# Moving start-up work of a convolution and feed-forward kernel between VectorE, GpSimd, TensorE and the load queue

## Chip, cores, metric

One Trainium2 chip (trn2), one of its cores. The metric is the device time of one execution in microseconds; the median of several runs is quoted. The kernel before took 696.43 us (696.14 to 696.79, 4 runs).

## The reference

`x` is 8 x 4096 x 192. Each channel is convolved causally along the sequence with 7 taps, the softmax of its head's 7 weights (8 heads of 24 channels). The result passes, as 32768 tokens of 192, through two matrix products with a swish between them.

```python
w = softmax(weight)                                 # 8 heads x 7 taps
x_unf = x_pad[:, arange(S)[:, None] + arange(7)]    # 7 causal positions
conv = einsum('hk,bskhg->bshg', w, x_unf)           # 32768 x 192
h = conv @ w_in                                     # 192 -> 2048
g = h * (1 / (1 + exp(-beta * h)))
out = g @ w_out                                     # 2048 -> 192
```

## The kernel before

The kernel works in stages. A stage handles one chunk of 512 tokens from each of two halves of the batch; the first chunk is cut into two stages of 256 tokens, so that work can begin early. In each stage TensorE runs 16 units: the first-layer products of stage `s` (`hidden`) and the second-layer products of stage `s-1` (`output`). ScalarE applies the swish to each unit. VectorE convolves for the stage after the next, 21 instructions per chunk (7 taps, 3 channel groups of 64), which are queued and popped between units. As g = silu(beta h) / beta, the division is folded into w_out, once, at the start.

The first two stages cannot wait for VectorE's convolution. Theirs is done on TensorE as seven matmuls per channel group, each with a diagonal matrix of one tap's weight (`diag`). The parts that matter (cuts marked):

```python
    steps = [(0, 0, TOK // 2), (0, TOK // 2, TOK // 2)]      # two half chunks
    steps += [(ch, 0, TOK) for ch in range(1, N_CH)]
    psum_h = ctx.enter_context(tc.tile_pool(name="psum_h", bufs=2, space=PSUM))
    psum_o = ctx.enter_context(tc.tile_pool(name="psum_o", bufs=2, space=PSUM))
    # ... cut
    def load_w_in(i):                          # GpSimd queue, cast to bf16
        cols = slice(i * FW, (i + 1) * FW)
        nc.gpsimd.dma_start(out=w_in_s[0:DG, :, cols],
            in_=moe_w_in[:, cols].rearrange("(c d) f -> d c f", c=NG))

    def copy_w_in(i):                          # second half of the partitions
        cols = slice(i * FW, (i + 1) * FW)
        nc.vector.tensor_copy(w_in_s[DG : 2 * DG, :, cols], w_in_s[0:DG, :, cols])
    # ... cut: prologue: fillers, head weights spread to channels, transposes,
    #          diag, the first half chunk's convolution
    def taps():                                # exact taps for VectorE's convolution
        pq = psum_o.tile([128, 2, TOK], FP32, name="po")[:, 0, 0 : NG * (K + 1)]
        spread(pq, sel, e8)                    # fp32: 6 records for 3 matmuls, 0.83 us
    # ... cut
    cast(2)
    for c in range(0, NF, 4):
        prep_w_out(c, 4)                       # nc.gpsimd.tensor_tensor: w_out / beta
    cast(3)
    # ... cut
    first_work = {                             # inserted after unit u of the first stage
        0: lambda: (first_xt(), taps()),
        2: lambda: (more(xt1_work)(), copy_w_in(1)),
        4: lambda: (more(xt1_work)(), copy_w_in(2)),
        6: lambda: (more(conv1_work)(), copy_w_in(3)),
        8: more(conv1_work),
        11: more(conv1_work),
    }
    pops = {1: 12, 2: 26}                      # VectorE taps issued per stage
```

## Time and profile before

| what | before |
|---|---|
| median time | 696.43 us |
| TensorE busy | 687.6 of 695.1 us |
| a unit in the steady stages (16 first-layer units and 16 second-layer blocks a stage) | 0.65 + 0.66 us |
| first activation of the first stage | 11.84 us |
| start of ScalarE's unbroken run (13th unit of the first stage) | 23.05 us |
| first activation of the third stage | 37.18 us |
| TensorE's end | 690.99 us |

The profile's first part gives busy time by engine. Of the kernel before:

```profile
PE 687.6 (99%) x11467; PEld 526.6 (76%) x11467; DVE 551.4 (79%) x938; ACT 580.0 (83%) x546; POOL 70.0 (10%) x83
```

TensorE is full. From the third stage on only its matmuls matter, and the change touches none of them. What can move is the start. The next view is ScalarE's timeline: start, length, engine, line, operation, shape, count, and in brackets how long the engine stood idle before the group and for whom.

```profile
11.84 0.69 ACT L402 ACTIVATE g<-ph,beta 128x512 bf16<-128x512 f32 x1 [0.37 <-PE ph L395]
13.49 2.55 ACT L402 ACTIVATE g<-ph,beta 128x512 bf16<-128x512 f32 x4 [0.97 <-PE ph L395]
16.25 1.27 ACT L402 ACTIVATE g<-ph,beta 128x512 bf16<-128x512 f32 x2 [0.21 <-PE ph L395]
18.09 1.43 ACT L402 ACTIVATE g<-ph,beta 128x512 bf16<-128x512 f32 x2 [0.57 <-PE ph L395]
20.30 1.97 ACT L402 ACTIVATE g<-ph,beta 128x512 bf16<-128x512 f32 x3 [0.78 <-PE ph L395]
23.05 13.11 ACT L402 ACTIVATE g<-ph,beta 128x512 bf16<-128x512 f32 x20 [0.78 <-PE ph L395]
37.18 1.11 ACT L402 ACTIVATE g<-ph,beta 128x1024 bf16<-128x1024 f32 x1 [1.02 <-PE ph L395]
```

Sixteen activations of 0.655 us make up the first stage. The five gaps between them sum to 3.31 us (0.97 + 0.21 + 0.57 + 0.78 + 0.78). Each follows work that `first_work` inserts on TensorE; with two PSUM buffers, `hidden` is never more than about one unit ahead. From 23.05 us on ScalarE runs without a gap through the whole second stage, and so does TensorE. Before 37.18 us it waits 1.02 us for the third stage. The chain of waits (start, length, engine, tile, line) shows what was late there:

```profile
15.81 0.96 DVE xt L346
...
16.80 3.05 DVE w_in_s L172 x2
...
19.88 2.92 DVE ct L376 x3
22.79 1.32 DVE ct L378 x2
...
32.66 3.98 DVE ct L378 x6
...
36.69 0.39 PE ph L395 x2
```

The chain runs on VectorE for 21 us: two copies of w_in, first taps, other taps. TensorE's last two matmuls of the third stage's first unit start at 36.69 us, when VectorE's last tap is ready. The two copies take 3.05 us, while one alone takes 0.69 us at 8.77 us: at 16.2 to 22.4 us GpSimd runs its four products for w_out:

```profile
16.22 6.16 POOL L352 TENSOR_TENSOR w_out_s<-w_out_raw,beta_r 128x768 bf16<-128x768 f32 x4 [2.48 <-DMA w_out_raw<-in_moe_w_out_dram]
```

### The profile page before, as it was taken

How to read it: one execution, taken by the hardware profiler on the slowest of the kernel's cores; microseconds unless marked ns; L12 is line 12 of the kernel's file. 1: busy time of each engine (PE TensorE's matmuls, PEld its weight loads, DVE VectorE, ACT ScalarE, POOL GpSimd, SP SyncE). 2: the span in 40 equal slices, each digit the busy share in tenths (PEclk: the TensorE clock that was granted, in tenths of full speed). 3: DMA queues.
4: the chain of work that ended last, by engine and by line, in shares of the span. 5: the costliest groups of instructions: out<-in, count | busy, mean ns of one | idle time of the engine just before them, and what ended most of it. 6: DMA issues, size and time to landing. Idle time of an engine off the chain costs nothing.

```text
span 695.1 us, 24865 instructions
## 1 busy us (share of the span) xinstructions
PE 687.6 (99%) x11467; PEld 526.6 (76%) x11467; DVE 551.4 (79%) x938; ACT 580.0 (83%) x546; POOL 70.0 (10%) x83
## 2 busy tenths in 40 slices
PE   9999999999999999999999999999999999999997
PEld 6867777777777777777777777777777777777777
DVE  5999998998777987777987777987778987777222
ACT  6898888888888888888888888888888888888881
POOL 7934455000000000000000000000000000000000
PEclk9999999999999999999999999999999999999999
DMA  9999999922232022222023222032222122211012
GB/s 193 144 159 159 168 177 171 123 63 70 54 65 71 27 68 72 47 70 70 26 71 70 49 70 70 25 71 70 48 71 55 40 70 71 48 48 48 25 48 70
DMA packets 181497, 54.57 MB, mean 79 GB/s; under 512 B 146432, under 2 KB 181072, under 8 KB 181392
## 3 DMA queue, kind: packets, MB, share of 16 engines
q0 software_dynamic: 98048, 14.89, 29.8%
q1 hardware_dynamic: 83296, 38.09, 23.9%
q8 instruction: 89, 1.46, 0.9%
q14 instruction: 16, 0.13, 0.1%
q10 hardware_dynamic: 48, 0.01, 0.0%
HBM read 28.98 MB, written 37.29 MB: 95 GB/s over the span
## 4 chain that ended last, share of the span: by engine, by line
PE 96%; DVE 3%; ACT 0%; issue 0%
PE po L442 48%; PE ph L395 46%; DVE ct L378 2%; PE ph L256 0%; DVE w_in_s L172 0%; DVE ct L376 0%; PE ph L205 0%; PE po L209 0%; PE po L243 0%; ACT g L402 0%; PE po L256 0%; DVE xt L346 0%; DVE osb L457 0%; DVE ct L327 0%; ACT xt_145 L269 0%
## 5 line engine op out<-in xcount | busy, mean ns | idle before, releaser
L402 ACT ACTIVATE g<-ph,beta 128x1024 bf16<-128x1024 f32 (+1 forms) x528 | 572.7, 1090 | 96.7 <-PE ph L395 92.6
L442 PEld LDWEIGHTS <-g 64*128 64x128 bf16 x8192 | 369.2, 94 | 101.9
L442 PE MATMUL po<-w_out_s,g 64*128 64x192 bf16 x8192 | 429.8, 243 | 0.0
L395 PE MATMUL ph<-ct,w_in_s 64*128 64x512 bf16 (+1 forms) x3168 | 426.2, 370 | 2.0 <-ACT g L402 1.1
L378 DVE SCALAR_TENSOR_TENSOR ct<-xt,cw,ct 128x512 bf16<-128x512 bf16 x558 | 379.4, 745 | 0.0
L395 PEld LDWEIGHTS <-w_in_s 64*128 64x128 bf16 x3168 | 162.5, 94 | 56.4 <-issue 2.9
L456 DVE COPY osb<-po 128x384 f32<-128x384 f32 x127 | 70.8, 558 | 126.9 <-PE po L442 120.7
L457 DVE TENSOR_TENSOR osb<-po,osb 128x384 f32<-128x384 f32 x129 | 71.5, 555 | 6.0 <-ACT osb L454 1.6
L95 POOL DMA_DIRECT2D xd<-in_x_dram x60 | 54.4, 909 | 46.1 <-DMA xd<-in_x_dram 42.3
L376 DVE TENSOR_SCALAR ct<-xt,cw 128x512 bf16<-128x512 bf16 x93 | 29.5, 372 | 0.0
L454 ACT COPY osb<-po 128x192 f32<-128x192 f32 x2 | 0.6, 320 | 9.9 <-PE po L442 9.9
L352 POOL TENSOR_TENSOR w_out_s<-w_out_raw,beta_r 128x768 bf16<-128x768 f32 x4 | 6.2, 1568 | 2.5 <-DMA w_out_raw<-in_moe_w_out_dram 2.5
L205 PE MATMUL ph<-zeros 128*128 128x512 bf16 x7 | 3.5, 623 | 1.3 <-DVE warm L129 1.3
L172 DVE COPY w_in_s<-w_in_s 64x1536 bf16<-64x1536 bf16 x4 | 4.4, 1121 | 0.1
L256 PE MATMUL po<-xt_145,diag 128*128 128x256 f32 x28 | 4.4, 296 | 0.0
L256 PEld LDWEIGHTS po<-xt_145,diag 128*128 128x128 f32 x28 | 3.6, 189 | 0.7 <-issue 0.6
L256 PEld LDWEIGHTS ph<-xt_145,diag 128*128 128x128 f32 x14 | 3.1, 327 | 0.6 <-ACT xt_145 L269 0.6
L256 PE MATMUL ph<-xt_145,diag 128*128 128x256 f32 x14 | 3.4, 427 | 0.1
L185 POOL DMA_DIRECT2D w_out_raw<-in_moe_w_out_dram x4 | 3.1, 771 | 0.3 <-DMA x1b<-in_x_dram 0.3
L295 ACT ACTIVATE ct<-po,rn 128x256 bf16<-128x256 f32 x1 | 0.5, 475 | 2.6 <-PE po L256 2.6
L165 POOL DMA_DIRECT2D w_in_s<-in_moe_w_in_dram x4 | 2.7, 669 | 0.0
L205 PEld LDWEIGHTS <-zeros 128*128 128x128 bf16 x7 | 0.8, 126 | 2.3 <-DVE warm L129 1.3
(51 smaller groups left out, 28.1 us busy)
## 6 DMA issues: line engine op xcount, KB each, us to landing
out_dram<-osb SPq DMA_DIRECT2D x60, 384.0 KB, 3.1
xd<-in_x_dram POOLq DMA_DIRECT2D x54, 198.0 KB, 14.5
w_out_raw<-in_moe_w_out_dram POOLq DMA_DIRECT2D x4, 384.0 KB, 9.4
out_dram<-osb SPq DMA_DIRECT2D x7, 192.0 KB, 3.7
xd<-in_x_dram POOLq DMA_DIRECT2D x6, 192.0 KB, 13.7
x_83<-in_x_dram SPq DMA_DIRECT2D x4, 192.0 KB, 2.9
w_in_s<-in_moe_w_in_dram POOLq DMA_DIRECT2D x4, 192.0 KB, 7.7
xt<-xd SPq DMA_TRANSPOSE x30, 5.1
```

The lines of the kernel that those rows point to most:

```text
L95: nc.gpsimd.dma_start(out=xd[r0:, :, h, :], in_=x_v[p, t0:t1, h, :].rearrange("t (c d) -> t c d", c=NG),)
L172: nc.vector.tensor_copy(w_in_s[DG : 2 * DG, :, cols], w_in_s[0:DG, :, cols])
L205: nc.tensor.matmul(pf[:, 0, :], zeros[:, 0:128], zeros, start=True, stop=True)
L256: nc.tensor.matmul(pv, diag[:, c, k, :], xt0[:, c, o : o + n], start=(k == 0), stop=(k == K - 1),)
L352: nc.gpsimd.tensor_tensor(w_out_s[:, c0 : c0 + n, :], w_out_raw[:, c0 : c0 + n, :], beta_r[:, c0 : c0 + n].unsqueeze(2).to_broadcast((128, ...
L376: nc.vector.tensor_scalar_mul(dst, src, scalar)
L378: nc.vector.scalar_tensor_tensor(out=dst, in0=src, scalar=scalar, in1=dst, op0=ALU.mult, op1=ALU.add)
L395: nc.tensor.matmul(ph[:, h, 0:n], w_in_s[rows, j, cols], cts[s][rows, j, 0:n], start=(j == 0), stop=(j == NG - 1),)
L402: nc.scalar.activation(gs[s][:, fc, :, 0:n], ph[:, :, 0:n], AF.Silu, scale=beta[:, fc : fc + 1])
L442: nc.tensor.matmul(po[:, r, b * D : (b + 1) * D], g[rows, fc, h, q * BLK : (q + 1) * BLK], w_out_s[rows, fc, :], start=(fc == 0), stop=(fc ...
L456: nc.vector.tensor_copy(dst, po[:, 0, cols])
L457: nc.vector.tensor_tensor(dst, po[:, 1, cols], dst, ALU.add)
```

## The change

Its stated parts are: w_out scaled on VectorE instead of GpSimd; the last two of four w_in pieces loaded for both halves of the partitions, so VectorE copies two pieces less; and one channel group of the second chunk convolved by diagonals on TensorE, so VectorE has 14 taps instead of 21 there. The diff also moves the insertions of the first stage (after units 1, 2, 5, 8, 11 instead of 2, 4, 6, 8, 11), makes the exact taps from one-pass fp32r matmuls of the residual, puts three small filler matmuls between the first spread matmuls, issues the casts of later chunks at other places, and pops VectorE's first taps after units 3 to 9 of the first stage (before: 6 to 15). The intent is to relieve VectorE, on which the chain runs until 36.7 us. Its core (cut):

```diff
-    for i in range(1, NW):
-        load_w_in(i)
+    load_w_in(1)
+    for i in range(2, NW):
+        for h in range(2):
+            load_w_in(i, h)
@@ prologue
-    spread(pc[:, 0, :], sel_r, e8r)
+    e8l = setup.tile([H, K + 1], FP32R)
+    nc.vector.tensor_tensor(e8l, e8, e8r.bitcast(FP32), ALU.subtract)
+    spread(pc[:, 0, :], sel_r, e8r, between=1)     # a 128-column filler before each
@@ exact taps
-        spread(pq, sel, e8)
+        spread(pq, sel_r, e8l)
+        nc.vector.tensor_tensor(ef, pq.rearrange("p (c k) -> p c k", c=NG), eu, ALU.add)
@@ second chunk, third channel group
+    def second_conv():
+        pv = psum_o.tile([128, 2, TOK], FP32, name="po")[:, 0, :]
+        for k in range(K):
+            o = HALO - PAD + k
+            nc.tensor.matmul(pv, diag[:, 2, k, :], xt1[:, o : o + TOK],
+                             start=(k == 0), stop=(k == K - 1))
+        nc.scalar.mul(cts[2][:, 2, :], pv, rn[:, 2:3])
@@ w_out
-        nc.gpsimd.tensor_tensor(
+        nc.vector.tensor_tensor(
@@ where it is inserted: (stage, unit)
-        2: lambda: (more(xt1_work)(), copy_w_in(1)),
-        4: lambda: (more(xt1_work)(), copy_w_in(2)),
-        6: lambda: (more(conv1_work)(), copy_w_in(3)),
-        8: more(conv1_work),
-        11: more(conv1_work),
+        (0, 1): lambda: (more(xt1_work)(), copy_w_in(1)),
+        (0, 2): more(xt1_work),
+        (0, 5): more(conv1_work),
+        (0, 6): lambda: cast(3),
+        (0, 8): more(conv1_work),
+        (0, 11): lambda: (prep_w_out(0), prep_w_out(4), more(conv1_work)()),
+        (0, 13): lambda: prep_w_out(8),
+        (0, 14): lambda: prep_w_out(12),
+        (0, 15): lambda: cast(4),
+        (1, 7): second_conv,
-    pops = {1: 12, 2: 26}
+    pops = {1: 10, 2: 24}
```

More of the change, by code (lines that the diff above doesn't have):

```diff
@@ L161, with load_w_in @@
     w_in_s = consts.tile([128, NG, F], BF16)
-    def load_w_in(i):
+    def load_w_in(i, h=0):
         cols = slice(i * FW, (i + 1) * FW)
         nc.gpsimd.dma_start(
-            out=w_in_s[0:DG, :, cols],
+            out=w_in_s[h * DG : (h + 1) * DG, :, cols],
             in_=moe_w_in[:, cols].rearrange("(c d) f -> d c f", c=NG),
@@ L201, with fill, spread @@
     pf = psum_h.tile([128, 2, TOK], FP32, name="ph")
-    def fill(n):
+    def fill(n, cols=TOK):
         for _ in range(n):
-            nc.tensor.matmul(pf[:, 0, :], zeros[:, 0:128], zeros, start=True, stop=True)
-    def spread(dst, sel, e8):
+            nc.tensor.matmul(
+                pf[:, 0, 0:cols], zeros[:, 0:128], zeros[:, 0:cols], start=True, stop=True
+            )
+    def spread(dst, sel, e8, between=0):
         for c in range(NG):
+            fill(between, 128)
             nc.tensor.matmul(
@@ L274 @@
     diag_v(1)
+    nc.vector.tensor_copy(x0b[:, HB:NB], x0[:, HB:NB])
     for k in range(K):
@@ L295 @@
             nc.scalar.mul(ct[:, c, 0:n0], pv, rn[:, c : c + 1])
-    beta_r = setup.tile([128, NF], FP32)
-    nc.vector.reciprocal(beta_r, beta)
-    nc.vector.tensor_copy(x0b[:, HB:NB], x0[:, HB:NB])
     cw = consts.tile([128, NG, K], FP32)
@@ L304, in taps @@
         pq = psum_o.tile([128, 2, TOK], FP32, name="po")[:, 0, 0 : NG * (K + 1)]
-        spread(pq, sel, e8)
-        pq = pq.rearrange("p (c k) -> p c k", c=NG)
+        spread(pq, sel_r, e8l)
+        ef = setup.tile([128, NG, K + 1], FP32)
+        nc.vector.tensor_tensor(ef, pq.rearrange("p (c k) -> p c k", c=NG), eu, ALU.add)
         rq = setup.tile([128, NG], FP32)
-        nc.vector.reciprocal(rq, pq[:, :, K])
+        nc.vector.reciprocal(rq, ef[:, :, K])
         nc.vector.tensor_tensor(
-            cw, pq[:, :, 0:K], rq.unsqueeze(2).to_broadcast((128, NG, K)), ALU.mult
+            cw, ef[:, :, 0:K], rq.unsqueeze(2).to_broadcast((128, NG, K)), ALU.mult
         )
@@ L333, in first_conv @@
             yield
+    xt1 = setup.tile([128, HALO + TOK], FP32R)
+    def second_conv():
+        pv = psum_o.tile([128, 2, TOK], FP32, name="po")[:, 0, :]
+        for k in range(K):
+            o = HALO - PAD + k
+            nc.tensor.matmul(
+                pv, diag[:, 2, k, :], xt1[:, o : o + TOK], start=(k == 0), stop=(k == K - 1)
+            )
+        nc.scalar.mul(cts[2][:, 2, :], pv, rn[:, 2:3])
     def second_xt():
@@ L343, in second_xt, with prep_w_out @@
                 nc.vector.tensor_copy(
-                    xt[:, :, HALO - PAD : HALO], xt0[:, :, HALO + TOK - PAD :]
+                    xt[:, 0:2, HALO - PAD : HALO], xt0[:, 0:2, HALO + TOK - PAD :]
                 )
-                nc.vector.tensor_copy(xt[:, :, HALO:], pt)
+                nc.vector.tensor_copy(xt[:, 0:2, HALO:], pt[:, 0:2, :])
+                nc.vector.tensor_copy(
+                    xt1[:, HALO - PAD : HALO], xt0[:, 2, HALO + TOK - PAD :]
+                )
+                nc.vector.tensor_copy(xt1[:, HALO:], pt[:, 2, :])
             yield
     w_out_s = consts.tile([128, NF, D], BF16)
-    def prep_w_out(c0, n):
-        nc.gpsimd.tensor_tensor(
-            w_out_s[:, c0 : c0 + n, :],
-            w_out_raw[:, c0 : c0 + n, :],
-            beta_r[:, c0 : c0 + n].unsqueeze(2).to_broadcast((128, n, D)),
+    beta_r = setup.tile([128, NF], FP32)
+    def prep_w_out(c):
+        if c == 0:
+            nc.vector.reciprocal(beta_r, beta)
+        nc.vector.tensor_tensor(
+            w_out_s[:, c : c + 4, :],
+            w_out_raw[:, c : c + 4, :],
+            beta_r[:, c : c + 4].unsqueeze(2).to_broadcast((128, 4, D)),
             ALU.mult,
@@ L359 @@
     cast(2)
-    for c in range(0, NF, 4):
-        prep_w_out(c, 4)
-    cast(3)
     def conv_ops(s):
@@ L380, in tap @@
                 )
-        return [lambda j=j, k=k: tap(j, k) for k in range(K) for j in range(NG)]
+        return [lambda j=j, k=k: tap(j, k) for k in range(K) for j in range(NG - (s == 2))]
     gs = {}
@@ L468 @@
     first_work = {
-        0: lambda: (first_xt(), taps()),
-        2: lambda: (more(xt1_work)(), copy_w_in(1)),
-        4: lambda: (more(xt1_work)(), copy_w_in(2)),
-        6: lambda: (more(conv1_work)(), copy_w_in(3)),
-        8: more(conv1_work),
-        11: more(conv1_work),
+        (0, 0): lambda: (first_xt(), taps()),
+        (0, 1): lambda: (more(xt1_work)(), copy_w_in(1)),
[8 more added lines that the diff above has]
+        (1, 7): second_conv,
     }
-    pops = {1: 12, 2: 26}
+    pops = {1: 10, 2: 24}
     queue = deque()
@@ L486 @@
                 output(s - 1, u)
-            if s == 0 and u in first_work:
-                first_work[u]()
+            if (s, u) in first_work:
+                first_work[s, u]()
             n = pops.get(s, 24)
-            pops_u = (u + 1) * n // NF - u * n // NF if s else u > 5
+            pops_u = (u + 1) * n // NF - u * n // NF if s else 2 < u < 10
             for _ in range(pops_u):
@@ L493 @@
                     queue.popleft()()
-            if u == 0 and s + 4 < N_CH:
+            if u == 0 and 0 < s < N_CH - 4:
                 cast(s + 4)
```

## The prediction

> **What bounds the kernel now.** TensorE: 687.6 of 695.1 us busy at granted clock 1.00 (busy table). In the steady stages a unit costs 0.65 us of first-layer and 0.66 us of second-layer matmuls without a wait (chain in order of time, from 53 us on). The change touches none of these; only the first 53 us can move. The timeline shows there:
> - 0 to 11.5 us, prologue. 14 conv taps by diagonals from 6.35 take 3.36 us, 7 later ones (16.5) 1.09; their weight loads fall from about 235 to 120 ns at about 10.2 us[...].
> - 11.5 to 25.1, first half chunk: 16 units of 0.655 us on ScalarE, idle 3.3 us in five gaps, each behind TensorE work (transposes, tap matmuls, conv) that two PSUM buffers cannot hide. VectorE delays TensorE little (0.42, 0.27, 0.45 us).
> - 25.1 to 35.6, second half: TensorE and ScalarE both full, 0.655 us a unit.
> - At 35.6 the third stage waits for VectorE's convolution: its first unit is done at 37.08 instead of about 36.23, costing 0.85 us. The chain runs on VectorE from 15.8 to 36.7.
>
> **The change.** VectorE, 15.8 to 36.7: two copies of w_in go (3.04 us, slowed by GpSimd; 0.69 alone), seven taps go (0.35 + 6 x 0.745 = 4.8 us), three first taps fall from 2.92 to about 1 us; four products of 128x768 come (estimate 0.9 each, from the 0.94 us product of that shape). Net about 6 us less: the wait at 35.6 vanishes, 0.85 us gained.
>
> TensorE: seven 512-column fp32r taps in the second half. A 256-column group inserts 1.18 us (16.36 to 17.54); 7 x 0.107 us more make 1.9 us, with ScalarE's scaling of about 0.67 us (from 0.475 us for half) about 2.05 us, all on the chain, as that stage has no slack. Kernel-tap matmuls in one pass instead of two: 0.4 us off. Transposes after units 1 and 2 instead of 2 and 4, waiting for a buffer: by my hand schedule ScalarE's gaps become 3.9 instead of 3.3 us. The three fillers cost up to 0.3 us[...]. The two added loads land near 15 to 17 us, before units 8 and 12; w_out lands 2.3 us later, still before its use.
>
> **Sum.** -0.85 + 2.05 + 0.6 + 0.3 = +2.1 if the clock rises as before[...]. As unseen scheduling gains are likely in a change placed this finely, I lean lower: predicted 697.4 us, 8 in 10 between 695.2 and 699.2. Faster by over 2%: 0.01; within 2%: 0.985; slower: 0.005.
>
> **What would show it.** No convolution wait at the start of the third stage; a hole of about 2 us in ScalarE's run near unit 7 of the second stage, with seven 512-column matmuls in about 1.8 us; w_out products near 0.9 us, first taps near 0.35; ScalarE's gaps in the first stage about 3.9 us; the 1.31 us steady unit unchanged; the first 14 conv taps 3.3 us (cold) or about 2 (warm).
>
> **What would make it wrong.** The clock rising earlier with DMA keeping up; w_out or w_in landing late on the longer GpSimd queue and stalling VectorE; ScalarE's gaps in the first stage shrinking; a wait for a PSUM buffer at unit 8 of the second stage, whose output tile reuses the one being emptied.

Three passages are cut, because they rest on what no trace or run here shows: why the weight loads get shorter, and, in the change and in the sum, that the fillers bring this forward. The sum came to +2.1 us, or to +0.9 with the terms that are cut (the first stage 0.9 us sooner instead of the fillers' 0.3 us); the four terms that stand give +2.1.

Measured numbers beside the rest: in the trace of before the first 14 taps start 213 ns apart and the next seven 120 ns, with weight loads of 330 and 190 ns. "Cold" and "warm" stand for taps before and after that fall, and the clock's rise for the moment at which a trace's clock record begins (9.90 us before); the 2 us for 14 warm taps is about twice the 1.09 us of seven. The 0.107 us for 256 more columns in a matmul became 0.103 us, (1.81 - 1.09) / 7 between the two traces; the one-pass matmuls saved 0.34 us of the 0.4 us said. The 0.3 us for the fillers is the estimate; what they cost is under after_again.

## The result

The changed kernel took 698.75 us (698.47 to 699.11, 4 runs) against 696.43 us: ratio 1.0033, 95% interval 1.0016 to 1.0051. It is slower, by about 2.3 us, though within 2%. A ratio here is the mean time of one kernel's fast runs over that of the other's of the same rounds, so it is not quite the ratio of the medians. Run once more beside others, the changed kernel gave 699.12 us and 1.0038 (1.0026 to 1.0051). Its output was correct, as was that of every kernel below.

Busy times of the changed kernel:

```profile
PE 689.0 (99%) x11474; PEld 528.8 (76%) x11474; DVE 547.1 (78%) x937; ACT 580.0 (83%) x547; POOL 65.1 (9%) x81
```

TensorE is busy 1.4 us longer, VectorE 4.3 us and GpSimd 4.9 us less: the work did leave them. ScalarE's timeline in the changed kernel:

```profile
11.98 0.69 ACT L424 ACTIVATE g<-ph,beta 128x512 bf16<-128x512 f32 x1 [0.37 <-PE ph L417]
13.30 0.69 ACT L424 ACTIVATE g<-ph,beta 128x512 bf16<-128x512 f32 x1 [0.63 <-PE ph L417]
14.46 0.69 ACT L424 ACTIVATE g<-ph,beta 128x512 bf16<-128x512 f32 x1 [0.47 <-PE ph L417]
15.35 1.97 ACT L424 ACTIVATE g<-ph,beta 128x512 bf16<-128x512 f32 x3 [0.20 <-PE ph L417]
18.08 1.97 ACT L424 ACTIVATE g<-ph,beta 128x512 bf16<-128x512 f32 x3 [0.77 <-PE ph L417]
20.83 1.97 ACT L424 ACTIVATE g<-ph,beta 128x512 bf16<-128x512 f32 x3 [0.79 <-PE ph L417]
23.59 7.85 ACT L424 ACTIVATE g<-ph,beta 128x512 bf16<-128x512 f32 x12 [0.79 <-PE ph L417]
32.89 0.69 ACT L351 ACTIVATE ct<-po,rn 128x512 bf16<-128x512 f32 x1 [1.45 <-PE po L348]
33.48 5.25 ACT L424 ACTIVATE g<-ph,beta 128x512 bf16<-128x512 f32 x8
39.08 1.11 ACT L424 ACTIVATE g<-ph,beta 128x1024 bf16<-128x1024 f32 x1 [0.35 <-PE ph L417]
```

The gaps of the first stage now sum to 3.65 us (0.63 + 0.47 + 0.20 + 0.77 + 0.79 + 0.79). The run that was unbroken is broken at 31.44 us: ScalarE waits 1.45 us for seven matmuls and then scales their result (0.69 us). The gap before the third stage is down from 1.02 to 0.35 us, the bare hand-over: only_second_conv and relief_split have 0.35 us there too. The chain of the changed kernel:

```profile
31.04 1.81 PE po L348 x7
...
38.33 0.65 PE ph L417 x6
```

It has left VectorE and runs on TensorE alone: the seven matmuls of the second convolution stand in it with 1.81 us, and the third stage starts with six matmuls in 0.65 us and no wait.

The loss can be split at events that both traces have. "First stage" is from the first activation to the start of the 13th, "second stage" from there to the third stage's first activation, "rest" from there to TensorE's end:

| us | first activation | first stage | second stage | rest | TensorE's end |
|---|---|---|---|---|---|
| before | 11.84 | 11.21 | 14.13 | 653.81 | 690.99 |
| changed | 11.98 | 11.61 | 15.49 | 653.80 | 692.88 |
| difference | +0.14 | +0.40 | +1.36 | -0.01 | +1.89 |

The trace of before is of a run of 696.80 us, that of the changed kernel of one of 698.71 us: their difference of 1.91 us is the traced one. The larger gap of 2.3 us between the medians comes from where other runs of each kernel fell. What their starts scatter with is seen under after_again. The rest of the kernel takes the same time to 0.01 us in both, and to 0.02 us in all but one of the kernels below, so only the first three columns need attention.

### The profile page after: what moved, and what is told of

Read it like the earlier page. It is cut to its first block, busy times and chain, and to the rows that moved or that the text cites. A ratio compares the mean times of both kernels' runs of the same rounds, so it can differ in the third digit from the quotient of the medians.

```text
span 697.0 us, 24878 instructions
## 1 busy us (share of the span) xinstructions
PE 689.0 (99%) x11474; PEld 528.8 (76%) x11474; DVE 547.1 (78%) x937; ACT 580.0 (83%) x547; POOL 65.1 (9%) x81
## 4 chain that ended last, share of the span: by engine, by line
PE 98%; ACT 1%; DVE 0%; issue 0%
PE po L464 48%; PE ph L417 48%; PE po L263 1%; ACT g L424 1%; PE ph L207 0%; PE ph L263 0%; PE po L250 0%; PE po L348 0%; DVE xt L323 0%; PE po L214 0%; ACT xt L276 0%; ACT ct L303 0%; DVE osb L479 0%; ACT osb L476 0%; DVE zeros L127 0%
## 5 line engine op out<-in xcount | busy, mean ns | idle before, releaser
L400 DVE SCALAR_TENSOR_TENSOR ct<-xt,cw,ct 128x512 bf16<-128x512 bf16 x552 | 375.4, 744 | 0.0
L398 DVE TENSOR_SCALAR ct<-xt,cw 128x512 bf16<-128x512 bf16 x92 | 27.4, 351 | 0.2 <-DMA xt<-xd 0.2
L207 PE MATMUL ph<-zeros 128*128 128x512 bf16 (+1 forms) x10 | 4.2, 524 | 1.3 <-DVE warm L129 1.3
L263 PE MATMUL po<-xt,diag 128*128 128x256 f32 x28 | 4.4, 296 | 0.0
L263 PEld LDWEIGHTS po<-xt,diag 128*128 128x128 f32 x28 | 3.6, 189 | 0.7 <-issue 0.6
L377 DVE TENSOR_TENSOR w_out_s<-w_out_raw,beta_r 128x768 bf16<-128x768 f32 x4 | 3.6, 952 | 0.0
L263 PEld LDWEIGHTS ph<-xt,diag 128*128 128x128 f32 x14 | 2.6, 285 | 0.6 <-ACT xt L276 0.6
L263 PE MATMUL ph<-xt,diag 128*128 128x256 f32 x14 | 2.8, 377 | 0.1
```

The source lines that it names most:

```text
L207: nc.tensor.matmul(pf[:, 0, 0:cols], zeros[:, 0:128], zeros[:, 0:cols], start=True, stop=True)
L263: nc.tensor.matmul(pv, diag[:, c, k, :], xt0[:, c, o : o + n], start=(k == 0), stop=(k == K - 1),)
L377: nc.vector.tensor_tensor(w_out_s[:, c : c + 4, :], w_out_raw[:, c : c + 4, :], beta_r[:, c : c + 4].unsqueeze(2).to_broadcast((128, 4, D) ...
L398: nc.vector.tensor_scalar_mul(dst, src, scalar)
L400: nc.vector.scalar_tensor_tensor(out=dst, in0=src, scalar=scalar, in1=dst, op0=ALU.mult, op1=ALU.add)
```

## Experiments

Twelve kernels ran, in three groups, each group on one chip with the kernel before in the same rounds, five rounds each. The two theories at the start: (A) the second convolution costs TensorE and ScalarE about 2 us in a stage where both are full and buys back under 1 us, and the places of the insertions cost a little more; (B) the loss is elsewhere, in the longer load queue, in VectorE's new work, or in the fillers.

| kernel | median us | ratio to before (95%) | first act. | first stage | second stage |
|---|---|---|---|---|---|
| no_second_conv | 698.31 | 1.0028 (1.0014 to 1.0041) | 11.72 | 11.60 | 14.48 |
| no_fill | 697.95 | 1.0026 (1.0013 to 1.0038) | 11.82 | 11.59 | 15.49 |
| old_places | 698.55 | 1.0028 (1.0015 to 1.0040) | 12.09 | 10.52 | 15.49 |
| only_second_conv | 699.32 | 1.0042 (1.0029 to 1.0054) | 12.28 | 12.47 | 15.51 |
| pool_w_out | 699.42 | 1.0042 (1.0029 to 1.0054) | 12.23 | 11.61 | 15.97 |
| old_places_no_conv | 696.52 | 0.9999 (0.9986 to 1.0013) | 12.55 | 10.55 | 13.79 |
| relief_only | 695.29 | 0.9988 (0.9975 to 1.0000) | 11.96 | 10.52 | 14.50 |
| relief_split | 699.60 | 1.0040 (1.0027 to 1.0053) | 12.04 | 10.43 | 17.53 |
| best | 695.54 | 0.9987 (0.9973 to 1.0001) | 11.20 | 10.86 | 13.78 |
| best_fill2 | 695.84 | 0.9986 (0.9973 to 0.9998) | 10.74 | 10.53 | 13.79 |
| only_fill | 696.28 | 1.0002 (0.9990 to 1.0015) | 11.80 | 10.79 | 14.03 |
| after_again | 699.12 | 1.0038 (1.0026 to 1.0051) | 12.44 | 11.60 | 15.49 |

The medians of before were 696.10, 696.46 and 696.57 us in the three groups. The three columns of stages come from one trace of each kernel, and that run need not be a typical one: it was the slowest of the five for no_fill, only_second_conv and relief_only, and the fastest for no_second_conv, old_places, best_fill2 and only_fill.

### no_second_conv

```diff
-        (1, 7): second_conv,
-        return [... for j in range(NG - (s == 2))]
+        return [... for j in range(NG)]          # VectorE has all 21 taps again
-    pops = {1: 10, 2: 24}
+    pops = {1: 15, 2: 26}
```

> The changed kernel with the third channel group of the second chunk given back to VectorE, all else kept. Theory A (the TensorE insertion of 1.94 us in the full second stage is the loss, and it buys back less than 0.9 us): the second stage shrinks to 10.5 us; VectorE ends its 21 taps near 36.9 us, so the third stage waits about 0.8 us and its first unit ends near 37.4 us (38.98 in the changed kernel, 37.08 before). Time about 1.6 us below the changed kernel, 0.2 to 0.4 above the kernel before. Rival B (without the seven taps moved, VectorE is several us late): first unit later than 38.5 us, time as the changed kernel or worse.

ScalarE and VectorE of this kernel around the third stage's start:

```profile
23.32 13.11 ACT L409 ACTIVATE g<-ph,beta 128x512 bf16<-128x512 f32 x20 [0.78 <-PE ph L402]
37.80 9.22 ACT L409 ACTIVATE g<-ph,beta 128x1024 bf16<-128x1024 f32 x9 [1.37 <-PE ph L402]
```

```profile
22.88 0.96 DVE L333 TENSOR_TENSOR ct<-po,rn 128x768 bf16<-128x768 f32 x1 [1.42 <-PE po L263]
...
25.48 4.06 DVE L385 SCALAR_TENSOR_TENSOR ct<-xt,cw,ct 128x512 bf16<-128x512 bf16 x6
30.81 0.56 DVE L463 COPY osb<-po 128x384 f32<-128x384 f32 x1 [1.26 <-PE po L449]
...
31.87 5.38 DVE L385 SCALAR_TENSOR_TENSOR ct<-xt,cw,ct 128x512 bf16<-128x512 bf16 x8
```

The second stage's run is unbroken again, 20 activations in 13.11 us. But VectorE's last tap ends at 37.25 us, and the gap is 1.37 us, that is 1.02 us more than the hand-over of 0.35 us; 0.8 us had been expected. The second stage is 1.01 us shorter than in the changed kernel (15.49 to 14.48), not the 1.6 us that theory A expected of the time. The ratio moved less still (1.0033 and 1.0038 to 1.0028): the intervals overlap, so only the trace tells the two kernels apart. Theory A has the right sign and too large a size: with the insertions and pops at these places VectorE needs much of what TensorE was given. It idles 1.42 us for the last first-stage convolution and 1.26 us for an output block, both in program order ahead of taps that were ready.

### no_fill

```diff
-    spread(pc[:, 0, :], sel_r, e8r, between=1)
+    spread(pc[:, 0, :], sel_r, e8r)              # residual of the taps computed later
```

> The changed kernel without the three small fillers between the spread matmuls, and with the residual of the taps computed later on VectorE. Theory A (fillers delay the first taps by 0.7 us but make the array clock rise about 0.9 us earlier, so they nearly cancel): taps start at 6.4 us instead of 7.06, the clock rises near 10 us again, the first activation near 11.85 instead of 11.98; time 0.1 to 0.2 us lower. Rival B (the clock's rise does not depend on the fillers): rise stays near 9.2 us, first activation near 11.3, time 0.7 us lower.

The stages are those of the changed kernel to 0.02 us. The first taps start at 6.35 us instead of 7.06, take 3.36 us instead of 2.85, and the first activation is at 11.82 instead of 11.98 us, the numbers of theory A. But after_again, the changed kernel itself, had its first activation at 12.44 us, so one pair of traces does not decide this; see there. (By the clock records, which begin at 9.90 us before and at 9.14 us in the changed kernel, the rise is 0.76 us earlier in that pair, not 0.9.) The ratio is not told apart from that of the changed kernel.

### old_places

```diff
-        (0, 1): lambda: (more(xt1_work)(), copy_w_in(1)),
-        (0, 2): more(xt1_work),
-        (0, 5): more(conv1_work),
-        (0, 6): lambda: cast(3),
+        (0, 2): lambda: (more(xt1_work)(), copy_w_in(1)),
+        (0, 4): more(xt1_work),
+        (0, 6): lambda: (more(conv1_work)(), cast(3)),
 # and VectorE's taps popped after units 5 to 11 instead of 3 to 9
```

> The changed kernel with the insertions of the first stage back after units 2, 4 and 6 (instead of 1, 2 and 5). Theory A (these places cost ScalarE about 0.4 us of idle time): the second stage starts near 25.25 us instead of 25.61, its gaps on ScalarE sum to about 3.3 instead of 3.65 us; time 0.3 to 0.4 us lower than the changed kernel. Rival B (the 0.4 us came from VectorE or the longer load queue): start stays near 25.6 us, time the same.

The first stage falls to 10.52 us, 1.08 us less than in the changed kernel where 0.4 had been expected, and its gaps to 2.73 us (0.63 + 0.21 + 0.58 + 0.53 + 0.78). Theory A's sign holds, its size does not, because two gains of the change were hidden under the new places: against the kernel before, the gap behind the exact taps fell from 0.97 to 0.63 us (one pass instead of two, 0.49 us of TensorE instead of 0.83), and one of the gaps of 0.78 us to 0.53, as unit 8 no longer waits for VectorE's copy of w_in (0.42 us in the traced run of the kernel before; only_fill, with the same copies, shows no such wait, so the second gain is not one of every run). The times moved less than the trace, as this kernel's runs fell in two groups, 697.70 and 697.73 us (the profiled one among them), and 698.55 to 698.59 us.

### only_second_conv

```diff
+            if (s, u) == (1, 7):
+                second_conv()                    # the kernel before, plus this alone
-    pops = {1: 12, 2: 26}
+    pops = {1: 10, 2: 24}
```

> The kernel before with only the second convolution by diagonals added, nothing else of the change. Theory A: insertion of 1.95 us in the second stage, the wait of 0.67 to 0.85 us at the third gone: time 1.1 to 1.4 us above the kernel before, that is more than half of the change's whole loss. Rival B (VectorE's relief there pays for the insertion): time equal to the kernel before within 0.3 us.

It is slower by 2.9 us. The second stage is 15.51 us, 1.38 us over the kernel before, which is what theory A expected. The other 1.26 us come in the first stage:

```profile
20.53 0.69 ACT L417 ACTIVATE g<-ph,beta 128x512 bf16<-128x512 f32 x1 [1.32 <-PE ph L410]
```

```profile
PE ph L410 <- DVE w_in_s L172: 1.4, 1, 1.4
```

TensorE waits 1.4 us for VectorE's copy of w_in. Laying out the third channel group in fp32r takes VectorE longer (four copies with 1.94 us in the changed kernel's trace, two with 1.13 us in that of before), and here the copy comes behind that and beside GpSimd's products. The trace is of the slowest of five runs (698.64 to 699.85 us), so this wait may be shorter in others. In the trace, then, the second convolution needs the loads for both halves, and the changed kernel shows that even with them it is a loss.

### pool_w_out

```diff
-        nc.vector.tensor_tensor(                 # the changed kernel, w_out / beta
+        nc.gpsimd.tensor_tensor(                 # on GpSimd again, after the casts
```

> The changed kernel with w_out scaled on GpSimd again, as before the change. Theory A (VectorE idles about 6 us in the changed second stage, so its 3.65 us of products are free there and their move to VectorE neither costs nor gains): time within 0.3 us of the changed kernel, 2.2 to 2.6 us above the kernel before; VectorE's first taps longer than the 0.35 us they take alone. Rival B (GpSimd's products hold VectorE up): first stage 0.5 us or more longer, time as much higher.

Theory A's number falls, by the trace: the second stage is 0.48 us longer than in the changed kernel. The times alone cannot say so, as the intervals overlap (1.0042 against 1.0033 and 1.0038). The rival has the cause right and the place wrong: the first stage, which it expected to be 0.5 us longer, is unchanged (11.61 us). In the groups by shape between 15 and 27 us, the columns after the bar are busy us and mean ns of one. First the changed kernel, then pool_w_out:

```profile
L400 DVE SCALAR_TENSOR_TENSOR ct<-xt,cw,ct 128x512 bf16<-128x512 bf16 x7 | 4.8, 742 | 0.0
L377 DVE TENSOR_TENSOR w_out_s<-w_out_raw,beta_r 128x768 bf16<-128x768 f32 x4 | 3.6, 952 | 0.0
L398 DVE TENSOR_SCALAR ct<-xt,cw 128x512 bf16<-128x512 bf16 x2 | 1.0, 545 | 0.0
```

```profile
L402 DVE SCALAR_TENSOR_TENSOR ct<-xt,cw,ct 128x512 bf16<-128x512 bf16 x7 | 8.4, 1256 | 0.0
L400 DVE TENSOR_SCALAR ct<-xt,cw 128x512 bf16<-128x512 bf16 x2 | 1.9, 973 | 0.0
```

The same seven taps take 1256 ns each instead of 742, the two first taps 973 instead of 545. Seven times 514 ns is 3.6 us, as much as VectorE's own four products cost (3.6 us). VectorE then delivers the second stage's input late, TensorE waits 0.7 us for it, and that is the longer second stage. GpSimd's products run here from 16.83 to 24.19 us, with a break of 0.8 us; the five taps beside and just after them take 7.03 us together, the next four 2.72 us. By what mechanism they slow VectorE no run shows. So scaling w_out on VectorE was a sound part of the change: about 3.6 us are paid on VectorE either way, and there they can be placed.

### old_places_no_conv

This kernel takes the edits of no_second_conv and old_places together, with `pops = {1: 12, 2: 26}` and VectorE's taps popped after units 5 to 15 of the first stage.

> The changed kernel with two parts undone: insertions after units 2, 4 and 6, and no second convolution on TensorE. Theory A (the two losses add, and VectorE with w_out's products ends its taps near 36.0 us): first stage from first activation to ScalarE's unbroken run 10.5 us as in old_places; the third stage still waits for VectorE about 1 us; from the first activation to TensorE's end about 678.6 us (679.15 before, 680.92 in the changed kernel); time 0.2 to 0.6 us below the kernel before. Rival B (VectorE is later than that): at or above the kernel before.

The first stage is 10.55 us and the second 13.79 us, 0.34 us shorter than before; from the first activation to TensorE's end it took 678.15 us, as expected within 0.5 us. Removing these two parts took 1.06 and 1.70 us off the changed kernel's stages, more together than the 1.01 us of no_second_conv might suggest: with these places and pops VectorE idles 0.19 us for the convolution instead of 1.42, and the gap before the third stage is 0.68 us. So these two parts are what makes the changed kernel lose: without them the stretch from the first activation to TensorE's end falls from 680.90 to 678.15 us, 1.00 us under the kernel before (679.15). The traced run is the median one, and in it the first activation came at 12.55 us, the latest of all, which takes back 0.71 us; the other runs were not traced.

### relief_only

```diff
 # on the kernel before
-    for i in range(1, NW):
-        load_w_in(i)                             # and copies 2 and 3 gone
+    load_w_in(1)
+    for i in range(2, NW):
+        for h in range(2):
+            load_w_in(i, h)
-        spread(pq, sel, e8)                      # exact taps in one pass
+        spread(pq, sel_r, e8l)
+    cast(3)                                      # ahead of GpSimd's products for w_out
```

> The kernel before with little of the change kept: the last two w_in pieces loaded for both halves, the exact taps in one pass, the second chunk's casts issued ahead of w_out's products, which stay on GpSimd; no fillers, old places, no second convolution. Theory A (loading w_in for both halves alone lifts enough off VectorE: its taps end near 32 us, before the second stage ends near 34.7): first stage 10.5 us, no wait for VectorE at the third stage; from first activation to TensorE's end about 677.5 us; time 1.4 to 1.9 us below the kernel before. Rival B (GpSimd's products slow VectorE so much that it is still late): wait at the third stage stays over 0.5 us, time at most 0.8 us below the kernel before.

About 0.8 us below before by the ratio, half of what theory A expected, with an interval that reaches 1. The five runs fall in two groups, 695.09 to 695.29 and 696.47 to 696.61 us, and the trace is of the slowest; what follows need not hold for the faster three, which are 1.2 to 1.4 us below the median of before. The first stage has its 10.52 us, and there is no wait for taps at the third stage. But with GpSimd's products still running, VectorE delivered the second stage's input late, and TensorE waited 1.2 us for it: the second stage takes 14.50 us. The rival had the cause right and the place wrong. The taps are slow here as in pool_w_out (three took 4.48 us beside the products), so it looks like the same effect.

### relief_split

```diff
-        (0, 6): more(conv1_work), (0, 8): more(conv1_work), (0, 11): ...
+        **{(0, u): more(conv1_work) for u in range(5, 14)},   # 2, 2, 3 taps each
```

> As relief_only, with the three convolutions of the first stage inserted as 2, 2 and 3 taps after each of the units 5 to 13, and the tap matmuls after unit 1 instead of 0. Theory A (by the hand schedule an insertion of X us costs ScalarE about X - 0.36 us, and seven taps at once are 1.18): ScalarE's idle sum in the first stage falls by about 0.9 us against relief_only, time as much lower. Rival B (each piece pays a fixed start cost that eats the gain): idle sum and time as relief_only or worse.

A clear failure, and the rival holds for the pieces. The 0.36 us was the estimate by a hand schedule. ScalarE's timeline and TensorE's waits:

```profile
17.05 0.69 ACT L413 ACTIVATE g<-ph,beta 128x512 bf16<-128x512 f32 x1 [0.18 <-PE ph L406]
...
27.44 0.69 ACT L413 ACTIVATE g<-ph,beta 128x512 bf16<-128x512 f32 x1 [1.85 <-PE ph L406]
28.58 0.69 ACT L413 ACTIVATE g<-ph,beta 128x512 bf16<-128x512 f32 x1 [0.45 <-PE ph L406]
29.86 0.69 ACT L413 ACTIVATE g<-ph,beta 128x512 bf16<-128x512 f32 x1 [0.59 <-PE ph L406]
```

```profile
PE ph L406 <- DVE ct L337: 2.3, 1, 2.3
```

Every piece now leaves a gap of 0.17 to 0.31 us. ScalarE's gaps sum to 2.74 us over the first stage, as much as relief_only's 2.72 us (0.63 + 0.21 + 0.57 + 0.53 + 0.78); behind the nine pieces alone they sum to 1.95 us, behind relief_only's three convolutions to 1.88. TensorE's own timeline shows 0.21 us of idle weight load ahead of each piece, which seven taps in a row pay once. Ahead of the bf16 transposes it stands idle as long, so the type of the matmul alone is not the cause; which cause it is, no run shows. The last piece also came after unit 13, so VectorE's scaling of it was late and TensorE waited 2.3 us. After that wait came a second loss. From 27.4 to 30.8 us, just after it, the granted clock in this trace is 0.50, and three units in a row took 1.14 to 1.28 us instead of 0.655, about 1.7 us more; that the wait brought the drop, one trace does not show. Four of the five runs have a mean clock of 0.996 or 0.997 and took 699.13 to 700.09 us; the fifth has 0.999 and took 698.08 us. So without the drop of the clock the split and its wait would cost about 1.6 us against the median of before, by that one run, which was not traced. The tap matmuls were moved by a unit as well, and no run separates that.

### best

This is old_places_no_conv with no_fill's edit: of the change it keeps w_out's products on VectorE, the loads for both halves, and the one-pass taps.

> old_places_no_conv without the fillers: w_out's products on VectorE and w_in's last pieces loaded for both halves kept from the change, the rest undone except the one-pass exact taps. Theory A (stages add): from first activation to TensorE's end 678.2 us as in old_places_no_conv, first activation near 11.85 us as in the kernel before; time 0.8 to 1.2 us below the kernel before, in the same rounds. Rival B (the fillers' earlier clock is worth something): first activation no earlier than with the fillers, time as the kernel before.

ScalarE's timeline of best (its first activation, its unbroken run and the third stage):

```profile
11.20 0.69 ACT L409 ACTIVATE g<-ph,beta 128x512 bf16<-128x512 f32 x1 [0.37 <-PE ph L402]
...
22.06 13.11 ACT L409 ACTIVATE g<-ph,beta 128x512 bf16<-128x512 f32 x20 [0.78 <-PE ph L402]
35.84 11.25 ACT L409 ACTIVATE g<-ph,beta 128x1024 bf16<-128x1024 f32 x11 [0.68 <-PE ph L402]
```

The second stage takes 13.78 us as in old_places_no_conv, with a gap of 0.68 us before the third; the first takes 10.86 us. The ratio is 0.9987 with an interval that just includes 1. From the first activation on, it took 678.45 us against 679.15 before and 680.90 in the changed kernel; the rest of its lead in the trace is a first activation at 11.20 us, which goes with an early rise of the clock (8.31 us; see after_again) and is luck as far as these runs show. So it beats the changed kernel by about 3.5 us, and the kernel before by about 0.9 us, at the edge of what these rounds can show.

### best_fill2

```diff
-    fill(1)                                      # just before the first taps
+    fill(2)
```

> best with one more 512-column filler just before the first taps. Theory A [...]: taps start 0.2 to 0.4 us later, clock rises earlier than 10 us; first activation equal or up to 0.4 us earlier, and the spread between runs smaller. Rival B (only delay): first activation 0.2 to 0.4 us later, time likewise.

The reason that theory A gave is cut, as no run shows it. The taps did not start later (6.35 us), against what both theories said: TensorE had been waiting for ScalarE's copy anyway. The 14 first taps took 2.32 us, the shortest of all, and the first activation was at 10.74 us. But the trace is of the fastest run, and the runs scatter more than those of best (694.78 to 695.98 against 695.26 to 695.86 us), where theory A expected less; so whether the filler did it stays open. The interval (0.9973 to 0.9998) just leaves 1 out, as one of twelve that were looked at; the ratio is that of best, and the two are not told apart.

### only_fill and after_again

> The kernel before with only the three small fillers between the spread matmuls. Theory A (delay of 0.6 us in the start of the taps and an earlier rise of the clock cancel): taps start near 6.95 us, clock up near 9.2 us; first activation within 0.3 us of the kernel before; time within 0.3 us. Rival B: time 0.5 us or more higher (delay alone) or lower (clock).

The first taps start at 7.07 instead of 6.35 us, the first 14 take 2.66 instead of 3.36 us, the first activation is at 11.80 us and the ratio 1.0002: in this run the taps' later start (0.72 us) and their shorter time (0.70 us) cancel, as theory A said of the sum. Its stages should be those of the kernel before, and are 10.79 and 14.03 us instead of 11.21 and 14.13: VectorE's two copies took 2.52 us instead of 3.04, no unit waited for them, and the gap before the third stage is 0.63 us, with 0.26 us earlier in that stage, instead of 1.02. So what the change could gain at these points differs from trace to trace by some tenths of a us.

> The changed kernel itself, once more beside the others on one chip: 2.2 to 2.6 us above the kernel before.

The ratio of 1.0038 (about 2.6 us) reproduces the first. Its trace has the stages of the first trace to 0.01 us, but a first activation at 12.44 instead of 11.98 us, with the same instructions. That scatter goes with the taps' speed. TensorE's timeline of the first 14 taps, in the changed kernel and then in after_again:

```profile
7.06 2.85 PE L263 MATMUL ph<-xt,diag 128*128 128x256 f32 x14
```

```profile
7.07 3.30 PE L263 MATMUL ph<-xt,diag 128*128 128x256 f32 x14
```

The same matmuls took 2.85 and 3.30 us. Their weight loads last 330 ns each at first and 190 ns later, and the change comes where the trace's clock record begins: at 9.14 us in the first trace and at 10.17 us in this one. (Earlier there is no record, and the views print 1.00 there.) What the clock was before that, the traces do not record, and why it rises at another time in an identical run, no run shows.

The record begins between 7.22 and 10.87 us in the fourteen traces, and the first activation follows it closely: about 0.42 us later for each us by which the clock rises later (best: 8.31 and 11.20 us; before: 9.90 and 11.84; only_second_conv: 10.87 and 12.28). Two straight lines, 7.73 + 0.417 r without the three fillers (seven traces) and 8.11 + 0.424 r with them (seven), where r is the time of the rise, give every first activation to 0.02 us. At the same rise, 9.8 us for example, the fillers thus delay the first activation by 0.45 us. Whether they bring the rise forward is not settled: it came at 8.31 to 10.87 us without them (best_fill2 left out) and at 8.51 to 10.51 us with them. The first activation came at 11.20 to 12.28 us without the fillers (mean of six, before included, best_fill2 left out: 11.86) and at 11.72 to 12.55 us with them (mean of seven: 12.12).

## Why the prediction was right

The time of 698.75 us lies in the predicted range of 695.2 to 699.2 us, within 2% as said. The mechanism of the main terms held, and luck helped two small ones:

| term of the sum | predicted | measured in the two traces |
|---|---|---|
| the third stage's wait for VectorE vanishes | -0.85 | -0.67 (gap 1.02 to 0.35) |
| second convolution inserted in a full stage | +2.05 | +2.03 (15.49 - 14.13 + 0.67) |
| places of the insertions, ScalarE's gaps | +0.6 | +0.40 for the stage, gaps 3.31 to 3.65 |
| fillers, if the clock rises as before | +0.3 | +0.14 (first activation, one pair of traces) |
| sum | +2.1 | +1.90 |
| leaning lower for gains not seen | -1.1 | none left in the sum |

The step that was off is the last: "As unseen scheduling gains are likely in a change placed this finely, I lean lower". The sum without it, about 698.5 us, was within 0.3 us of the result; the headline of 697.4 us was 1.35 us off. No run showed a gain of that kind beyond the terms above.

Two of the agreements are partly luck. The +0.40 us of the first stage is a remainder: old_places shows that the new places cost 1.09 us (10.52 to 11.61), while the other parts, the one-pass taps and the w_in loads among them, had gained 0.69 us (11.21 to 10.52). And the +0.14 us of the fillers is one draw: the second trace of the same kernel would give +0.60. At the same rise of the clock the fillers cost 0.45 us.

The signs that the prediction named came as said: no wait at the third stage; a hole of about 2 us in ScalarE's run (1.45 us idle and 0.69 us scaling) beside seven 512-column matmuls in 1.81 us; products at 0.95 us; ScalarE's gaps at 3.65 instead of the said 3.9 us; the steady unit unchanged. The first taps took 0.55 us instead of 0.35. On the fillers it left two cases open, cold or warm; the truth was a bit of both, 2.85 us for the 14 taps, and differs from run to run. Its reading of the clock was somewhat off: in the trace of before the weight loads last 330 and then 190 ns (the taps start 213 and then 120 ns apart, not 235 and 120), and the clock's record begins at 9.90 us, not at 10.2.

Of the rivals, the longer load queue cost nothing seen: no wait on w_in or w_out after the change. One thing that the prediction did not see is that the taps themselves, not only copies and first taps, slow down beside GpSimd's products (pool_w_out: 1256 ns against 742). In the kernel before they had run mostly after those products, so its trace did not show it.

Still open: whether the fillers, or one more before the taps, lift the clock earlier, and why the runs of relief_only and some others fall in two groups about 1 us apart.

## What to carry to other kernels

When an engine is late at one point, moving its work to an engine that is full at that point costs the whole length of the work and gains at most the wait; here 2.0 us were paid for 0.7. Look first at what merely slows the late engine: here copies that a DMA could do, another engine at work beside it (taps of 1256 instead of 742 ns), and instructions in program order ahead of ready work. Undo a change's parts one by one and also in pairs, for gains can be hidden under another part's loss, and compare stages between common events when the start scatters by as much as the effect. Read the granted clock after a long wait of TensorE: in relief_split it stood at 0.50 for 3.4 us after a wait of 2.3 us, and about half of the loss in the trace came from there.
